# Attention scores in three float32r passes from the second batch on, with scores and exponentials in a tile per head

## The chip, the cores and the metric

The kernel runs on one core of a Trainium2 chip. The metric is the device time of one execution in microseconds (us); lower is better. The core's engines each work through their own queue in order and meet only where one waits for another: TensorE (PE in the rows; PEld is its weight load, which overlaps PE), VectorE (DVE), ScalarE (ACT), GpSimd (POOL), and the queue that issues nearly all DMAs (SP).

## What is computed

Masked attention over 4 batches of 8 heads (576 positions, head size 64), and after it two feed-forward stages over the 2304 tokens, all in float32 with float32 accuracy:

```python
scores = scale * np.matmul(q, k.transpose(0, 1, 3, 2))
thresh = np.max(scores, axis=-1, keepdims=True) - tau
scores = np.where(scores >= thresh, scores, -1e9)
scores = scores - np.max(scores, axis=-1, keepdims=True)
attn = np.exp(scores)
attn = attn / (np.sum(attn, axis=-1, keepdims=True) + 1e-09)
x = np.matmul(attn, v)            # then to (2304, 512)
x = ((x @ w1) * (x @ w2)) @ w3 @ w_out
h = x @ w_in
out = np.maximum(0.01 * h, h) @ w2_out
```

## The kernel before

Two heads are handled together, one in SBUF partitions 0 to 63 and one in 64 to 127. A *unit* is such a pair of heads with about half of its queries: group 0 has 256 queries in 2 steps of 128, group 1 has 320 in 3 steps, of which the first (`c is None`) holds 64 queries of either head in one block through the zero-padded tile `qz`. There are 32 units, 8 to a batch, and 80 steps.

In step `n` the loop at L463 records: `mask(n)` (DVE: keep what lies above the threshold, and sum), `scores(n + 1)` (PE: q times k, two halves of 288 keys for either head, into the PSUM tile `sc`; then, head by head, the negated maximum `nm` and the threshold `th` on DVE and the exponential `e` on ACT), `weighted` for the unit before (PE: `av`), `transposes(n)` (PE: `tp`, `tq` for head 0 and head 1; ACT copies head 0 into `HH`, DVE copies head 1), and `normalise` for the unit before (PE: `bc`; DVE: `xs`; ACT and POOL split `xs` into a float32r pair `x`). Between these stand pieces of a *filler*: `fold_weights` (`ps`, L361) in the first batch, then `gated` (L370) for the group that was finished last, 24 pieces of 12 matmuls: 16 of `psab` (L383), 8 of `psh` (L402). `rate` sets how many pieces a step gets. After the last step come the rest of `gated` and the second feed-forward stage (`up`, `down`).

The feed-forward matmuls take float32 accuracy from three float32r passes over split operands (`PASSES`: high by high, high by low, low by high). The scores, transposes, `av`, `bc` and the folding run in float32; there the compiler makes two instructions of each matmul. A scores matmul uses 64 of the array's 128 rows: head 0 the upper half, head 1 the lower.

What sets the order: PE's is as recorded up to the end of the attention, SP's as recorded up to the middle of batch 1; DVE, ACT, POOL and later SP are ordered by the scheduler. `sc` is a single tile of four PSUM banks for both heads, with one buffer; `e` is one tile for both heads, with two. `scale_unit(u + 1)` runs on DVE in the last step of unit `u`, between `mask(n)` and `scores(n + 1)`. `load_unit(u + 2)` in the first step of unit `u` issues the DMAs of `qk` and `vv`, three buffers each. `ps_w` has two PSUM banks, through which `psab`, `psh`, `av` and `bc` take turns.

Of the kernel before, what the change touches and what calls it, by code (L numbers as in the profile page):

```python
# [33 lines left out]
    (b * 4 + p, g, c) for b in range(B) for g in range(2) for p in range(4) for c in CHUNKS[g])  # L34
NS = len(STEPS)
PASSES = ((0, 0), (0, 1), (1, 0))


@with_exitstack
def attention_gated_ffn(ctx: ExitStack, tc: tile.TileContext, qkv, tau, w3t, wout, w12, w2, out):  # L40
# [32 lines left out]
    nc.vector.memset(sides[D:, D:], 1.0)  # L73
    qz = [cpool.tile([P, P], F32, name=f"qz{i}") for i in range(2)]
    tl = [apool.tile([P, 2, 320], F32, name=f"tl{i}") for i in range(2)]
    for t in (*qz, *tl):
        nc.vector.memset(t, 0.0)
    one = cpool.tile([P, 1], F32, name="one")
    nc.vector.memset(one, 1.0)
# [20 lines left out]
    def stream(jobs, by_dve):  # L100
# [13 lines left out]
        def issue(most=2 * len(jobs)):  # L114

            while len(loaded) < min(most, len(todo)):
                (slot, src, raw), c = todo[len(loaded)]
                if len(loaded) >= state[0] + (7 if raw in ("wB", "wC") else 3):
                    return
                if raw is None:  # L120
                    st = wld.tile([P, 1024], I32, tag="st", name="st", bufs=3)
                    nc.sync.dma_start(out=st, in_=src[:, c * 512:c * 512 + 512].bitcast(I32))
                    loaded.append(st)
                else:
                    if c == 0:
# [37 lines left out]
    def load_unit(u):  # L163

        if u >= len(units):
            return
        pair, g = units[u]
        gq, gw, _ = GROUPS[g]
        b, h = pair // 4, 2 * (pair % 4)
        qk = apool.tile([P, S + 320], F32, tag="qk", name="qk", bufs=3)  # L170
        vv = apool.tile([P, 2, NK, D], F32, tag="vv", name="vv", bufs=3)
        for a in range(2):
            o = a * D
            src = qkv[b, h + a][o:o + D]
            if g == 0:
                nc.sync.dma_start(out=qk[o:o + D, :S + gw], in_=src[:, :S + gw])
            else:
                nc.sync.dma_start(out=qk[o:o + D, :S], in_=src[:, :S])
                nc.sync.dma_start(out=qk[o:o + D, S:], in_=src[:, S + gq:2 * S])
        for a in range(2):  # L180
            nc.sync.dma_start(
                out=vv[:, a], in_=qkv[b, h + a][:, 2 * S:].rearrange("p (c d) -> p c d", c=NK))
        qk_t[u], vv_t[u] = qk, vv

    def scale_unit(u):

        if u >= len(units):
            return
        g = units[u][1]
        qk = qk_t[u]  # L190
        if g:
# [7 lines left out]
            nc.vector.tensor_scalar(out=q, in0=q, scalar1=scl, scalar2=None, op0=ALU.mult))  # L199


    sc_t, e_t, stat = {}, {}, {}

    def scores(n):
# [4 lines left out]
        heads = range(1 if c is None else 2)  # L209
        sc = ps_a.tile([P, 2, 2, 512], F32, tag="sc", name="sc")  # L210
        for half in range(2):
            ks = slice(half * HS, half * HS + HS)
            for a in heads:
                if c is None:
                    nc.tensor.matmul(sc[:, a, half, :HS], qz[u % 2], qk[:, ks], start=True, stop=True)
                else:
                    r = slice(a * D, a * D + D)
                    o = S + Q0[c] - GROUPS[g][0]
                    nc.tensor.matmul(sc[:, a, half, :HS], qk[r, o:o + P], qk[r, ks], start=True, stop=True)  # L219
        e = apool.tile([P, 2, S], F32, tag="e", name="e", bufs=2)  # L220
        ths = []
        for a in heads:
            nm = apool.tile([P, 1], F32, tag="nm", name="nm", bufs=4)
            th = apool.tile([P, 1], F32, tag="th", name="th", bufs=4)
            nc.vector.tensor_reduce(out=nm, in_=sc[:, a, :, :HS], op=ALU.max, axis=AX.XY, negate=True)  # L225
            nc.vector.tensor_scalar(out=th, in0=nm, scalar1=-1.0, scalar2=cb, op0=ALU.mult, op1=ALU.add)
            nc.scalar.activation(  # L227
                e[:, a].rearrange("p (a b) -> p a b", a=2), sc[:, a, :, :HS], AF.Exp, bias=nm)
            ths.append(th)
        sc_t[n], e_t[n] = (sc, ths), e  # L230

    def mask(n):
# [5 lines left out]
        for a, th in enumerate(ths):  # L238
            ev = e_t[n][:, a].rearrange("p (a b) -> p a b", a=2)
            o = 4 if c is None else 2 * (c % 2) + a  # L240
            nc.vector.scalar_tensor_tensor(  # L241
                out=ev, in0=sc[:, a, :, :HS], scalar=th, in1=ev, op0=ALU.is_ge, op1=ALU.mult,
                accum_out=stat[key][:, o:o + 1])
# [3 lines left out]
    def transposes(n):  # L247
# [21 lines left out]
        for a in range(2):  # L269
            tp = ps_a.tile([P, 4, P], F32, tag="tp", name="tp")  # L270
            for kc in range(4):
                nc.tensor.transpose(tp[:, kc], e[:, a, kc * P:kc * P + P], ident)  # L272
# [4 lines left out]
            nc.tensor.transpose(tq[:, a], e[:, a, S - P:], ident)  # L277
            if a:
# [184 lines left out]
    for n in range(NS):  # L463
# [205 lines left out]
```

## Time and profile before

| | |
|---|---|
| median of 3 runs | 1104.95 us (1103.55 to 1105.52) |
| the profiled execution | 1104.54 us, of which the span from first to last instruction is 1102.7 |
| busy share of the span | PE 97%, DVE 46%, ACT 43%, POOL 23% |
| attention | from the start to about 645 us (folding in the first 125 us) |
| end of the gated stage and second feed-forward stage | from there to the end |

A row of a timeline begins with the start in us and the duration in us, then engine, line, operation, output tile, arrow, inputs, shape; in square brackets stands how long the engine had been idle before it and what ended that. Rows that follow one another on one engine are merged, with their count behind an x. A matmul's duration holds its way through the array, so that consecutive ones overlap; what one costs is the distance from start to start.

### The profile page before, as it was taken

To read this page: it belongs to the slowest core of one execution; us is meant where nothing else is said; L and a number is where in the kernel's file an instruction comes from. 1 tells how busy PE (TensorE), PEld (TensorE's weight loads), DVE (VectorE), ACT (ScalarE), POOL (GpSimd) and SP (SyncE) were. 2 spreads that over 40 slices of the span, in tenths; PEclk is the share of its full clock that TensorE was granted. 3 is DMA by queue.
4 is the path that set the end of the run, shared out by engine and by line. 5 is a ranking of instruction groups with operands and counts; after the bars stand their busy time and mean duration, and the time that the engine had idled before them with its cause. 6 is when DMAs were issued, how large, how long until landed. Compare 5 with 4: busy or idle time off the path is not lost.

```text
span 1102.7 us, 16185 instructions
## 1 busy us (share of the span) xinstructions
PE 1065.0 (97%) x6368; PEld 864.2 (78%) x6368; DVE 508.8 (46%) x1087; ACT 474.0 (43%) x891; POOL 256.8 (23%) x256
## 2 busy tenths in 40 slices
PE   7999799999998999999999999999999999999998
PEld 5555487789877888877898789877888888888887
DVE  5767766554666555664556633365311211111111
ACT  4767744343444444443444443477422222222232
POOL 2536712021211120120212146477400100000000
PEclk7999899999999999998999999999999999999999
DMA  9654610312112212111120023356200110010010
GB/s 305 199 198 130 204 54 23 81 35 65 40 40 63 59 30 65 44 54 51 38 62 25 1 79 114 102 191 201 72 13 1 34 34 1 5 44 1 1 39 20
DMA packets 35099, 77.59 MB, mean 70 GB/s; under 512 B 4560, under 2 KB 19408, under 8 KB 32976
## 3 DMA queue, kind: packets, MB, share of 16 engines
q1 hardware_dynamic: 34880, 76.56, 22.0%
q8 instruction: 50, 0.82, 0.3%
q14 instruction: 25, 0.20, 0.1%
q10 hardware_dynamic: 144, 0.00, 0.0%
HBM read 67.11 MB, written 9.44 MB: 69 GB/s over the span
## 4 chain that ended last, share of the span: by engine, by line
PE 81%; DVE 7%; ACT 6%; DMA 2%; issue 2%; POOL 1%; ACTq 0%; SPq 0%; DVEq 0%; POOLq 0%
PE psab L383 16%; PE po L606 16%; PE ps L584 16%; PE psh L402 9%; PE av L294 7%; PE sc L219 7%; PE tp L272 4%; PE ps L361 4%; DVE e L241 2%; ACT e L227 1%; DVE t L145 1%; ACT t L142 1%; PE tq L277 1%; ACT lw L144 1%; ACT HH L276 1%
## 5 line engine op out<-in xcount | busy, mean ns | idle before, releaser
L383 PE MATMUL psab<-x,w 128*128 128x256 f32 (+1 forms) x1536 | 234.5, 303 | 2.9 <-DVE xs L325 2.0
L383 PEld LDWEIGHTS psab<-x,w 128*128 128x128 f32 x1536 | 208.9, 189 | 24.9 <-issue 15.9
L584 PE MATMUL ps<-h,w 128*128 128x512 f32 (+1 forms) x960 | 215.7, 370 | 0.4 <-POOL w L153 0.3
L606 PE MATMUL po<-w,gg 128*128 128x512 f32 x864 | 213.8, 392 | 1.8 <-ACT gg L591 1.8
L584 PEld LDWEIGHTS ps<-h,w 128*128 128x128 f32 x960 | 169.0, 188 | 36.3 <-POOL w L153 1.3
L606 PEld LDWEIGHTS po<-w,gg 128*128 128x128 f32 x864 | 159.2, 188 | 38.1 <-ACT gg L591 3.3
L592 DVE TENSOR_TENSOR gg<-gf,gg 128x512 fp32r<-128x512 f32 (+1 forms) x80 | 61.2, 765 | 270.0 <-ACT gg L591 268.4
L225 DVE TENSOR_REDUCE nm<-sc 128x1 f32<-128x576 f32 x144 | 108.8, 756 | 108.3 <-PE sc L219 66.7
L227 ACT ACTIVATE e<-sc,nm 128x576 f32<-128x576 f32 x144 | 107.0, 743 | 117.3 <-DVE nm L225 117.0
L589 ACT ACTIVATE gf<-ps 128x512 f32<-128x512 f32 (+1 forms) x80 | 44.2, 554 | 227.0 <-PE ps L584 227.0
L241 DVE SCALAR_TENSOR_TENSOR e<-sc,th,e 128x576 f32<-128x576 f32 x144 | 112.7, 815 | 46.5 <-ACT e L227 46.5
L402 PE MATMUL psh<-gt,w 128*128 128x256 f32 (+1 forms) x768 | 115.1, 301 | 0.6 <-ACT ht L409 0.5
L394 POOL TENSOR_TENSOR gt<-at,gt 128x256 fp32r<-128x256 f32 (+1 forms) x64 | 52.7, 824 | 264.3 <-ACT gt L393 264.3
L402 PEld LDWEIGHTS psh<-gt,w 128*128 128x128 f32 x768 | 104.1, 189 | 7.7 <-issue 5.4
L219 PE MATMUL sc<-qk 64*128 64x288 f32 x512 | 81.7, 438 | 15.1 <-DVE e L241 11.2
L272 PE MATMUL tp<-ident,e 128*128 128x128 f32 x512 | 79.1, 278 | 6.0 <-ACT HH L276 6.0
L272 PEld LDWEIGHTS tp<-ident,e 128*128 128x128 f32 x512 | 61.9, 143 | 16.2 <-ACT HH L276 8.5
L151 POOL TENSOR_TENSOR lw<-t,lw 128x512 int32<-128x512 int32 x48 | 66.0, 1380 | 25.6 <-ACT lw L144 15.2
L219 PEld LDWEIGHTS sc<-qk 64*128 64x128 f32 x512 | 44.9, 188 | 33.9 <-issue 9.5
L294 PE MATMUL av<-HH,vv 128*64 128x256 f32 (+1 forms) x512 | 69.8, 416 | 0.0
L561 POOL TENSOR_TENSOR h<-hr,h 128x1024 fp32r<-128x1024 f32 (+1 forms) x10 | 23.8, 2380 | 188.2 <-DVE h L560 188.2
L361 PE MATMUL ps<-wo,w 128*128 128x512 f32 x128 | 60.0, 614 | 5.3 <-DVE xs L325 4.7
(72 smaller groups left out, 989.0 us busy)
## 6 DMA issues: line engine op xcount, KB each, us to landing
st<-in_w SPq DMA_DIRECT2D x40, 512.0 KB, 4.6
vv<-in_qkv SPq DMA_DIRECT2D x64, 160.0 KB, 2.4
raw<-in_w3t SPq DMA_DIRECT2D x8, 1024.0 KB, 5.8
qk<-in_qkv SPq DMA_DIRECT2D x32, 208.0 KB, 3.5
qk<-in_qkv SPq DMA_DIRECT2D x32, 144.0 KB, 3.0
out<-os SPq DMA_DIRECT2D x18, 256.0 KB, 2.1
raw<-in_wout SPq DMA_DIRECT2D x4, 1024.0 KB, 11.3
raw<-in_w SPq DMA_DIRECT2D x4, 1024.0 KB, 6.2
```

What stands on the lines that cost most here:

```text
L151: nc.gpsimd.tensor_tensor(out=lw, in0=t, in1=lw, op=ALU.add)
L219: nc.tensor.matmul(sc[:, a, half, :HS], qk[r, o:o + P], qk[r, ks], start=True, stop=True)
L225: nc.vector.tensor_reduce(out=nm, in_=sc[:, a, :, :HS], op=ALU.max, axis=AX.XY, negate=True)
L227: nc.scalar.activation(e[:, a].rearrange("p (a b) -> p a b", a=2), sc[:, a, :, :HS], AF.Exp, bias=nm)
L241: nc.vector.scalar_tensor_tensor(out=ev, in0=sc[:, a, :, :HS], scalar=th, in1=ev, op0=ALU.is_ge, op1=ALU.mult, accum_out=stat[key][:, o:o ...
L272: nc.tensor.transpose(tp[:, kc], e[:, a, kc * P:kc * P + P], ident)
L294: nc.tensor.matmul(av[a * D:a * D + D, :gw], vv[:, a, kc], rhs, start=(i == 0), stop=(i == NK - 1))
L361: nc.tensor.matmul(ps, w3_t[i][:, j * P:j * P + P], wo_t[j // 2][:, (j % 2) * 512:(j % 2) * 512 + 512], start=(j == 0), stop=(j == KF - 1))
L383: nc.tensor.matmul(ps[:, :gw], w12_t[i][:, a, mat * 512 + kk * P:mat * 512 + kk * P + P], xt[kk][:, c, :gw], start=(m == 0), stop=(m == 11))
L402: nc.tensor.matmul(ps[:, :gw], w34_t[i // 2][:, a, i % 2, o * P:o * P + P], gt[i][:, c, :gw], start=(m == 0), stop=(m == 23))
L584: nc.tensor.matmul(ps[:, :tw], w2_t[j][:, a, kk * P:kk * P + P], h3_t[ci][:, c, kk, :tw], start=(m == 0), stop=(m == 11))
L606: nc.tensor.matmul(po_t[t], gg[:, c, t * P:t * P + P], w2_t[j][:, a, 512:], start=(j == 0 and (a, c) == PASSES[0]), stop=(j == KF2 - 1 and ...
```

## The change

- `sc` and `e` become one tile per head (`sc0`, `sc1` with two banks each; `e0`, `e1`).
- Units 0 to 7 (batch 0) compute scores as before. From unit 8 on, the scores are three float32r passes: `split_unit(u + 1)`, recorded in the first step of unit `u` behind `scores(n + 1)`, scales q on DVE, copies k and q to the float32r tile `qkh` on ScalarE, subtracts to `qkl` on VectorE, and for group 1 makes four 64x64 copies into `qzs`. `scale_unit` does nothing for these units.
- `qkh` and `qkl` share the ring `st` of the weight stage, which goes from 3 buffers to 4. `xpool` goes from 8 to 6, `vv` from 3 to 2 (loaded by `load_v`, one unit later than before), and `hr` is loaded in four pieces of 512 columns a chunk instead of two of 1024. `qz` moves to another pool.

The diff without the unchanged surroundings and the purely mechanical renames:

```diff
+PER = 8
-    xpool = ...tc.tile_pool(name="xpool", bufs=8, reuse_waits="tile"))
+    xpool = ...tc.tile_pool(name="xpool", bufs=6, reuse_waits="tile"))
-    qz = [cpool.tile([P, P], F32, name=f"qz{i}") for i in range(2)]
+    qz = [apool.tile([P, P], F32, name=f"qz{i}") for i in range(2)]
+    qzs = [apool.tile([P, 2, P], F32R, name=f"qzs{i}") for i in range(2)]
+    for t in qzs:
+        nc.vector.tensor_copy(t, tl[0][:, :, :P])
-                    st = wld.tile([P, 1024], I32, tag="st", name="st", bufs=3)
+                    st = wld.tile([P, 1024], I32, tag="st", name="st", bufs=4)
...
+    def load_v(u):
...
+        vv = vv_t[u] = apool.tile([P, 2, NK, D], F32, tag="vv", name="vv", bufs=2)
...
     def scale_unit(u):
-        if u >= len(units):
+        if u >= PER:
             return
...
+    def split_unit(u):
+        if not PER <= u < len(units):
+            return
+        g = units[u][1]
+        n = S + GROUPS[g][1]
+        qk = qk_t[u]
+        q = qk[:, S:n]
+        tc.keep_in_program_order(
+            nc.vector.tensor_scalar(out=q, in0=q, scalar1=scl, scalar2=None, op0=ALU.mult))
+        hi = wld.tile([P, 1024], F32R, tag="st", name="qkh", bufs=4)
+        lo = wld.tile([P, 1024], F32R, tag="st", name="qkl", bufs=4)
+        nc.scalar.copy(hi[:, :n], qk[:, :n])
+        nc.vector.tensor_tensor(out=lo[:, :n], in0=qk[:, :n], in1=f(hi[:, :n]), op=ALU.subtract)
+        qks_t[u] = (hi, lo)
+        if g:
+            for i, part in enumerate((hi, lo)):
+                for a in range(2):
+                    r = slice(a * D, a * D + D)
+                    nc.vector.tensor_copy(qzs[u % 2][r, i, r], part[r, S:S + D])
...
-        sc = ps_a.tile([P, 2, 2, 512], F32, tag="sc", name="sc")
+        sc = [ps_a.tile([P, 2, 512], F32, tag=f"sc{a}", name="sc") for a in heads]
+        if u < PER:
+            parts, qzu = (qk,), qz[u % 2].unsqueeze(1)
+        else:
+            parts, qzu = qks_t[u], qzs[u % 2]
+        passes = PASSES[:1] if u < PER else PASSES
         for half in range(2):
             ks = slice(half * HS, half * HS + HS)
-            for a in heads:
...
+            for i, (x, y) in enumerate(passes):
+                for a in heads:
+                    if c is None:
+                        lhs, rhs = qzu[:, x], parts[y][:, ks]
+                    else:
+                        r = slice(a * D, a * D + D)
+                        o = S + Q0[c] - GROUPS[g][0]
+                        lhs, rhs = parts[x][r, o:o + P], parts[y][r, ks]
+                    nc.tensor.matmul(
+                        sc[a][:, half, :HS], lhs, rhs, start=(i == 0), stop=(i == len(passes) - 1))
-        e = apool.tile([P, 2, S], F32, tag="e", name="e", bufs=2)
+        e = [apool.tile([P, S], F32, tag=f"e{a}", name="e", bufs=2) for a in heads]
...
             scores(n + 1)
+        if n and STEPS[n - 1][:2] != (pair, g):
+            split_unit(u + 1)
...
         if n == 0 or STEPS[n - 1][:2] != (pair, g):
+            load_v(u + 1)
             load_unit(u + 2)
...
-        for o in range(0, KD, 2):
-            hr = p2.tile([P, 2, 512], F32, tag="hr", name="hr")
+        for o in range(KD):
+            hr = p2.tile([P, 512], F32, tag="hr", name="hr")
```

PE, at the turn from batch 2 to batch 3, in the one step of a batch for which the filler has run out (`tp`, `tq`: transposes; `bc`: normalise; `sc`: scores of the next step; `av`: weighted). Before:

```order
L402 MATMUL psh<-gt,w_813 128x256 x6
L402 MATMUL psh<-gt,w_1013 128x256 x6
L272 MATMUL tp<-ident,e 128x128 x4
L277 MATMUL tq<-ident,e 128x128
L272 MATMUL tp<-ident,e 128x128 x4
L277 MATMUL tq<-ident,e 128x128
L322 MATMUL bc<-pairs,rb 128x64
L324 MATMUL bc<-ident,rb 128x128 x2
L219 MATMUL sc<-qk 128x288 x4
L294 MATMUL av<-tl_95,vv 64x256 x2
```

The same place after the change:

```order
L313 MATMUL tp<-ident,e 128x128 x4
L318 MATMUL tq<-ident,e 128x128
L363 MATMUL bc<-pairs,rb 128x64
L365 MATMUL bc<-ident,rb 128x128 x2
L259 MATMUL sc<-qkh 128x288 x2
L259 MATMUL sc<-qkl,qkh 128x288 x2
L259 MATMUL sc<-qkh,qkl 128x288 x2
L259 MATMUL sc<-qkh 128x288 x2
L259 MATMUL sc<-qkl,qkh 128x288 x2
L259 MATMUL sc<-qkh,qkl 128x288 x2
L335 MATMUL av<-tl_95,vv 64x256 x2
```

Nothing has moved around the scores; their four matmuls (eight instructions) have become twelve single ones, and the two of each row are head 0 and head 1.

DVE at the turn from batch 1 to batch 2, the step without filler and the one ahead of it (`nm`, `th`, `e,stat`: maximum, threshold and mask of a head; `rr`: reciprocals; `HH`: the copy of head 1's transposes). Before:

```order
L241 SCALAR_TENSOR_TENSOR e,stat<-sc,th,e 128x576 x2
L199 TENSOR_SCALAR qk<-qk,scl 128x256
L305 TENSOR_SCALAR rr<-stat 128x4
L306 RECIPROCAL rr<-rr 128x4
L274 COPY HH<-tp 128x4x128
L225 TENSOR_REDUCE nm<-sc 128x1
L226 TENSOR_SCALAR th<-nm,cb 128x1
L225 TENSOR_REDUCE nm<-sc 128x1
L226 TENSOR_SCALAR th<-nm,cb 128x1
L274 COPY HH<-tp 128x4x128
L241 SCALAR_TENSOR_TENSOR e,stat<-sc,th,e 128x576 x2
L325 TENSOR_TENSOR xs<-xs,bc 128x320
```

After, the same two steps:

```order
L267 TENSOR_SCALAR th<-nm,cb 128x1 x2
L222 TENSOR_SCALAR qk<-qk,scl 128x256
L282 SCALAR_TENSOR_TENSOR e,stat<-sc,th,e 128x576 x2
L226 TENSOR_TENSOR qkl<-qk,qkh 128x832
L346 TENSOR_SCALAR rr<-stat 128x4
L347 RECIPROCAL rr<-rr 128x4
L315 COPY HH<-tp 128x4x128
L266 TENSOR_REDUCE nm<-sc 128x1 x2
L267 TENSOR_SCALAR th<-nm,cb 128x1 x2
L282 SCALAR_TENSOR_TENSOR e,stat<-sc,th,e 128x576 x2
L315 COPY HH<-tp 128x4x128
L366 TENSOR_TENSOR xs<-xs,bc 128x320
```

The two maxima now stand side by side, the masks stand ahead of the copy of head 1, and the subtraction `qkl` stands behind the masks of the step before.

SP at the end of the attention (`st`: weights of the second stage; `hr`: the first chunk of its input). Before:

```order
L410 DMA h3d<-ht 128x256 x3
L559 DMA hr<-h3d 128x2x512
L122 DMA st<-in_w 128x1024 x2
L410 DMA h3d<-ht 128x256
L559 DMA hr<-h3d 128x2x512
```

After:

```order
L126 DMA st<-in_w 128x1024 x4
L451 DMA h3d<-ht 128x256 x3
L604 DMA hr<-h3d 128x512
L126 DMA st<-in_w 128x1024 x2
L451 DMA h3d<-ht 128x256
L604 DMA hr<-h3d 128x512
L126 DMA st<-in_w 128x1024 x2
L604 DMA hr<-h3d 128x512
```

The first loads of `st`, which before were issued early in the attention, now stand at its end, and the input comes in smaller pieces.

## Rows read from the trace of the kernel before

**Rows 1.** First part of the page: busy time, share of the span, instructions.
```profile
PE 1065.0 (97%) x6368; PEld 864.2 (78%) x6368; DVE 508.8 (46%) x1087; ACT 474.0 (43%) x891; POOL 256.8 (23%) x256
```

**Rows 2.** Busy time by stretch; then granted clock, DMA share, GB/s.
```profile
core 0: us, PE busy (x) PEld busy (x) DVE busy (x) ACT busy (x) POOL busy (x), PEclk, DMA share, GB/s
...
200.00:250.00 50.00, 47.68 (x336) 39.42 (x335) 27.74 (x65) 21.00 (x41) 9.39 (x12) 0.97 0.25 68
...
500.00:550.00 50.00, 47.68 (x327) 39.27 (x328) 26.88 (x63) 19.95 (x40) 9.39 (x12) 0.93 0.13 37
```

**Rows 3.** Waits of PE: for whom, us in total, times, longest.
```profile
PE sc L219 <- DVE e L241: 11.2, 8, 2.5
PE tp L272 <- ACT HH L276: 6.0, 7, 2.2
...
PE psab L383 <- DVE xs L325: 2.0, 8, 0.3
```

**Rows 4.** Timeline of PE at the turn from batch 2 to batch 3.
```profile
501.46 1.24 PE L219 MATMUL sc<-qk 64*128 64x288 f32 x8
502.63 1.70 PE L402 MATMUL psh<-gt,w 128*128 128x256 f32 x12
...
505.45 0.66 PE L272 MATMUL tp<-ident,e 128*128 128x128 f32 x4 [0.57 <-ACT HH L276]
...
506.22 0.39 PE L324 MATMUL bc<-ident,rb 128*128 128x128 f32 x2
508.36 2.29 PE L219 MATMUL sc<-qk 64*128 64x288 f32 x8 [1.75 <-DVE e L241]
```

**Rows 5.** Timelines of DVE and of ACT in the same step.
```profile
502.75 0.76 DVE L225 TENSOR_REDUCE nm<-sc 128x1 f32<-128x576 f32 x1 [2.02 <-PE sc L219]
...
504.32 0.76 DVE L225 TENSOR_REDUCE nm<-sc 128x1 f32<-128x576 f32 x1 [0.56 <-ACT e L227]
...
506.14 0.69 DVE L274 COPY HH<-tp 128x512 f32<-128x512 f32 x1 [0.82 <-PE tp L272]
506.75 0.81 DVE L241 SCALAR_TENSOR_TENSOR e<-sc,th,e 128x576 f32<-128x576 f32 x1
...
507.48 0.81 DVE L241 SCALAR_TENSOR_TENSOR e<-sc,th,e 128x576 f32<-128x576 f32 x1
...
505.29 0.75 ACT L227 ACTIVATE e<-sc,nm 128x576 f32<-128x576 f32 x1
```

**Rows 6.** Timeline in batch 1, a step ahead of a 64-query step.
```profile
298.03 1.22 PE L215 MATMUL sc<-qk,qz 128*128 128x288 f32 x4
...
298.96 0.48 DVE L325 TENSOR_TENSOR xs<-xs,bc 128x320 f32<-128x320 f32 x1
...
299.50 1.70 PE L383 MATMUL psab<-x,w 128*128 128x256 f32 x12 [0.25 <-DVE xs L325]
```

**Rows 7.** Full-height matmuls: float32 (timeline), float32r (chain that ended last).
```profile
98.17 3.60 PE L361 MATMUL ps<-wo,w 128*128 128x512 f32 x8
...
671.75 14.35 PE psab L383 x96
```

**Rows 8.** DVE and ACT operations nearest to the added ones (timeline; groups).
```profile
657.27 0.68 DVE L153 TENSOR_TENSOR w<-lw,w 128x512 fp32r<-128x512 f32 x1
...
L327 ACT CAST x<-xs 128x320 fp32r<-128x320 f32 x14 | 6.4, 460 | 25.4 <-DVE xs L325 25.1
L327 ACT CAST x<-xs 128x256 fp32r<-128x256 f32 x12 | 4.9, 407 | 13.3 <-DVE xs L325 13.3
...
L194 DVE TENSOR_SCALAR qz<-qk,scl 64x64 f32<-64x64 f32 x26 | 6.4, 248 | 0.4
```

**Rows 9.** Timelines of DVE and POOL behind the attention: the input's first chunk.
```profile
656.66 0.69 DVE L560 CAST h<-hr 128x1024 fp32r<-128x1024 f32 x1 [2.39 <-DMA hr<-h3d]
...
664.35 1.42 DVE L560 CAST h<-hr 128x1024 fp32r<-128x1024 f32 x1 [1.54 <-DMA hr<-h3d]
...
657.49 2.75 POOL L561 TENSOR_TENSOR h<-hr,h 128x1024 fp32r<-128x1024 f32 x1 [0.79 <-DVE h L560]
```

More of the change, by code (lines that the diff above doesn't have):

```diff
@@ L59, in attention_gated_ffn @@
     s_att = ExitStack()
-    xpool = s_ffn.enter_context(tc.tile_pool(name="xpool", bufs=8, reuse_waits="tile"))
+    xpool = s_ffn.enter_context(tc.tile_pool(name="xpool", bufs=6, reuse_waits="tile"))
     s_ld = ExitStack()
@@ L170, in load_unit @@
         qk = apool.tile([P, S + 320], F32, tag="qk", name="qk", bufs=3)
-        vv = apool.tile([P, 2, NK, D], F32, tag="vv", name="vv", bufs=3)
         for a in range(2):
@@ L179, in load_unit @@
                 nc.sync.dma_start(out=qk[o:o + D, S:], in_=src[:, S + gq:2 * S])
+        qk_t[u] = qk
+    def load_v(u):
+        if u >= len(units):
+            return
+        pair = units[u][0]
+        b, h = pair // 4, 2 * (pair % 4)
+        vv = vv_t[u] = apool.tile([P, 2, NK, D], F32, tag="vv", name="vv", bufs=2)
         for a in range(2):
@@ L182, in load_unit @@
                 out=vv[:, a], in_=qkv[b, h + a][:, 2 * S:].rearrange("p (c d) -> p c d", c=NK))
-        qk_t[u], vv_t[u] = qk, vv
     def scale_unit(u):
-        if u >= len(units):
+        if u >= PER:
             return
@@ L199, in scale_unit @@
             nc.vector.tensor_scalar(out=q, in0=q, scalar1=scl, scalar2=None, op0=ALU.mult))
+    qks_t = {}
+    def split_unit(u):
+        if not PER <= u < len(units):
+            return
+        g = units[u][1]
[14 more added lines that the diff above has]
+                    nc.vector.tensor_copy(qzs[u % 2][r, i, r], part[r, S:S + D])
     sc_t, e_t, stat = {}, {}, {}
@@ L209, in scores @@
         heads = range(1 if c is None else 2)
-        sc = ps_a.tile([P, 2, 2, 512], F32, tag="sc", name="sc")
+        sc = [ps_a.tile([P, 2, 512], F32, tag=f"sc{a}", name="sc") for a in heads]
[4 more added lines that the diff above has]
+        passes = PASSES[:1] if u < PER else PASSES
         for half in range(2):
             ks = slice(half * HS, half * HS + HS)
-            for a in heads:
[L214 to L219, printed above, removed]
-        e = apool.tile([P, 2, S], F32, tag="e", name="e", bufs=2)
+            for i, (x, y) in enumerate(passes):
[9 more added lines that the diff above has]
+        e = [apool.tile([P, S], F32, tag=f"e{a}", name="e", bufs=2) for a in heads]
         ths = []
@@ L224, in scores @@
             th = apool.tile([P, 1], F32, tag="th", name="th", bufs=4)
-            nc.vector.tensor_reduce(out=nm, in_=sc[:, a, :, :HS], op=ALU.max, axis=AX.XY, negate=True)
+            nc.vector.tensor_reduce(out=nm, in_=sc[a][:, :, :HS], op=ALU.max, axis=AX.XY, negate=True)
             nc.vector.tensor_scalar(out=th, in0=nm, scalar1=-1.0, scalar2=cb, op0=ALU.mult, op1=ALU.add)
             nc.scalar.activation(
-                e[:, a].rearrange("p (a b) -> p a b", a=2), sc[:, a, :, :HS], AF.Exp, bias=nm)
+                e[a].rearrange("p (a b) -> p a b", a=2), sc[a][:, :, :HS], AF.Exp, bias=nm)
             ths.append(th)
@@ L238, in mask @@
         for a, th in enumerate(ths):
-            ev = e_t[n][:, a].rearrange("p (a b) -> p a b", a=2)
+            ev = e_t[n][a].rearrange("p (a b) -> p a b", a=2)
             o = 4 if c is None else 2 * (c % 2) + a
             nc.vector.scalar_tensor_tensor(
-                out=ev, in0=sc[:, a, :, :HS], scalar=th, in1=ev, op0=ALU.is_ge, op1=ALU.mult,
+                out=ev, in0=sc[a][:, :, :HS], scalar=th, in1=ev, op0=ALU.is_ge, op1=ALU.mult,
                 accum_out=stat[key][:, o:o + 1])
@@ L260, in transposes @@
             for kc in range(4):
-                nc.tensor.transpose(tp[:, kc], e[:, 0, kc * P:kc * P + P], ident)
-            nc.tensor.transpose(tq[:, 0], e[:, 0, S - P:], ident)
+                nc.tensor.transpose(tp[:, kc], e[0][:, kc * P:kc * P + P], ident)
+            nc.tensor.transpose(tq[:, 0], e[0][:, S - P:], ident)
             nc.scalar.copy(HH[:, :, :, :D], tp.rearrange("p k (a w) -> p k a w", a=2))
@@ L271, in transposes @@
             for kc in range(4):
-                nc.tensor.transpose(tp[:, kc], e[:, a, kc * P:kc * P + P], ident)
+                nc.tensor.transpose(tp[:, kc], e[a][:, kc * P:kc * P + P], ident)
             if a:
@@ L276, in transposes @@
                 nc.scalar.copy(HH[:, :, a, o:o + P], tp)
-            nc.tensor.transpose(tq[:, a], e[:, a, S - P:], ident)
+            nc.tensor.transpose(tq[:, a], e[a][:, S - P:], ident)
             if a:
@@ L425, in attention_gated_ffn @@
     issue(2)
+    load_v(0)
     load_unit(1)
@@ L555, in load_h3 @@
         hh = pool.tile([P, 2, KD, 512], F32R, tag=f"h3{ci % 2}", name="h3", bufs=1)
-        for o in range(0, KD, 2):
-            hr = p2.tile([P, 2, 512], F32, tag="hr", name="hr")
-            hv = hr[:, :, :tw]
-            nc.sync.dma_start(out=hv, in_=h3d[o:o + 2, :, t0:t0 + tw].rearrange("o p t -> p o t"))
-            nc.vector.tensor_copy(hh[:, 0, o:o + 2, :tw], hv)
+        for o in range(KD):
+            hr = p2.tile([P, 512], F32, tag="hr", name="hr")
+            hv = hr[:, :tw]
+            nc.sync.dma_start(out=hv, in_=h3d[o, :, t0:t0 + tw])
+            nc.vector.tensor_copy(hh[:, 0, o, :tw], hv)
             nc.gpsimd.tensor_tensor(
-                out=hh[:, 1, o:o + 2, :tw], in0=hv, in1=f(hh[:, 0, o:o + 2, :tw]), op=ALU.subtract)
+                out=hh[:, 1, o, :tw], in0=hv, in1=f(hh[:, 0, o, :tw]), op=ALU.subtract)
         h3_t[ci] = hh
```

## The prediction, made before the changed kernel ran

> **What bounds the kernel now.** I read the page's busy times first, then the stretches, then PE's waits, and last the timelines around the longest of them. The page says that PE is busy for 97% of the span, and no other engine for half of it [rows 1]: time is saved where PE's instructions get shorter, or where PE stands idle or slow. In the attention's later batches DVE is busy 27.7 us of 50, ACT 21.0 [rows 2], so work added there can hide unless PE waits for just that instruction. PE's own waits are short but sit at fixed places [rows 3]: 11.2 us in 8 waits of the scores for a mask, 6.0 us of the transposes for a copy, 2.0 us in 8 of `psab` for `xs`. The timelines show why. At the turn of a batch the filler is used up; PE then has only transposes and `bc`, which are done at 506.6, and stands until 508.36, because the next scores overwrite `sc`, which the masks still read [rows 4]. The masks are that late because the two heads go one after the other: the second maximum waits for the exponential of the first (504.32, idle 0.56 behind ACT), the second exponential runs from 505.29 to 506.04, a copy stands ahead of the masks at 506.14, and the second mask ends at 508.3 [rows 5]. Both stretches with PE at 47.7 of 50 us hold such a turn, and in both the granted clock is below one, 0.97 and 0.93 [rows 2].
>
> **The change part by part.** All sums go against the profiled execution's 1104.54 us.
>
> *Scores of two heads, 48 steps.* A step's eight instructions take 1.17 us from start to start of the next (501.46 to 502.63) [rows 4]. Full-height float32 needs 3.60 us for eight instructions over 512 columns [rows 7], 0.45 each; that is two clocks a column at 2.4 GHz (0.427) and a tail, so 0.24 for 288 columns. Eight one after the other would be 1.92; 1.17 is four times 0.24 and 0.21. So the two heads, on either half of the array, run side by side, and I read the 0.21 as the change from full to half height and back. After the change there are six such pairs. Full-height float32r takes 14.35 us for 96 instructions over 320 columns [rows 7], 0.149 each including the tail, where one clock a column is 0.133; that gives 0.12 for 288 columns with nothing on top and 0.136 with it. I take 0.135, as the nearest row is a real stream: 6 x 0.135 + 0.21 = 1.02, 0.15 less than 1.17, **-7.2 us** in 48 steps. With 0.12 it is -11.5; the other end is the third rival.
>
> The Trainium skill ("FP8 and Floating Point Precision", TensorE Precision Notes) counts four passes for true float32, against the three passes here. By that ratio the 0.96 becomes 0.72, which is -11.5 us and a total of 1083; the float32r row with its 0.015 on top is why I stay above it.
>
> *Scores of 64 queries, 12 steps.* Four full-height float32 instructions of 0.24 become six of 0.135: -0.15 each, **-1.8 us**. Behind them `psab` waits for `xs`, 0.25 us each time [rows 6]; the eight waits make 2.0 us [rows 3]. DVE loses the two `qz` scalings of 0.248 us [rows 8] and a `scale` ahead of `xs` there, and its masks come earlier, so I take the six of batches 1 to 3 as gone: **-1.5 us** (0 if DVE fills the room otherwise).
>
> *One tile per head.* The maximum of head 1 needs no exponential any more, and the order shows both maxima, both thresholds, both masks and only then the copy. In the step of [rows 5]: first maximum at 502.6 (the scores are 0.15 shorter), second to 504.2, its exponential to 504.95, masks to 506.1. ACT copies head 0's transposes only behind both exponentials, so the second group of transposes starts at 505.6 and not 505.45, and `bc` ends at 506.75. The scores start there in place of 508.36: 1.6 us, of which 0.15 is counted above. What is late next is that copy on ACT, not DVE. Three turns: **-4.4 us**. Of the 11.2 us the turns are 3 x 1.75, and the longest single wait is 2.5, in the first steps, where I count nothing. The other four hold 3.5 us and are each shorter than what the masks gain (about 1.5): **-3.0 us**.
>
> *Clock.* 0.97 and 0.93 of 50 us are 1.5 and 3.5 us of lost array time [rows 2], behind the turns' idle stretches; the level there is 1.2 GHz. With idle times of about 0.9 us in place of 0.57 + 1.75 [rows 4] I expect most of it back: **-3.0 us** (0 to -5.0).
>
> *Splitting k and q, 24 units.* The nearest DVE subtraction takes 0.68 us for 512 columns [rows 8], so at most 1.1 and 1.2 us for 832 and 896. Four 64x64 copies cost up to 4 x 0.248, the two scalings they replace are saved. That is +1.1 us (group 0) and +1.7 us (group 1) a unit. ACT's cast grows by 53 ns in 64 columns, 407 to 460 [rows 8], hence 0.9 us. In all 34 us on DVE and 22 us on ACT, an eighth more for DVE in the attention. They stand behind masks and exponentials that PE needs, and ahead of `rr`, the product of `psab` and the copy of head 1. PE has `av` and a filler piece there, and DVE was idle 2.02 us before the next maximum [rows 5]. With all of it hidden the cost is 0, with all exposed 34; I take 0.1 a unit, **+2.4 us**. The scaling itself leaves the path between the last mask of a unit and the next unit's scores.
>
> *Smaller rings.* `vv` waits for the same `weighted` as before, now ahead of `qk` on SP; `qk` is wanted a unit later, so nothing waits. `xpool` with 6 holds a group of four and two of the next; the third is written when two thirds of `gated`, hence all of `psab`, are through. `st` is now held by `qkh` and `qkl`, so the first loads for the second stage move from early on to the end of the attention; SP's pieces of the input stand behind them. That input took 7.7 us from cast to cast for 1024 columns [rows 9]: about 4 of DMA, 0.7 of cast, 2.75 of POOL. Four half pieces repeat the DMA, up to 8 us more until the last, while PE has `psab` between: **+1.0 us** (0 to 8). The first batch keeps its instructions; 0 there, give or take 3.
>
> *Sum:* -7.2 -1.8 -1.5 -4.4 -3.0 -3.0 +2.4 +1.0 = -17.5, so 1087.0 for the profiled execution; the median of the runs lies 0.4 above that, **1087.4 us**.
>
> **The rivals.** *The waits stay* (the scheduler's order or ACT's copy holds PE all the same, so the tile per head doesn't do what it says): -7.2 -1.8 +3.4 gives 1098.9, with the median's 0.4 **1099**. Against it: the order has the masks ahead of the copy. *DVE becomes what PE waits for* in the split's steps: half of 1.4 us exposed in 24 units is 16.8 in place of 2.4, **1102**. For it speaks the unbroken block of two maxima, scaling, two masks, subtraction; against it the idle time of DVE. *Half-height float32r doesn't run side by side*: no row shows two such instructions at one clock a column. Twelve at 0.135 and 0.21 are 1.83 a step, +31.7 us in place of -7.2, so **1126**, slower. It decides from a pair of 0.196 us on, where 48 x (6 x 0.196 + 0.21 - 1.17) uses up the other gains of 10.3. Against it: float32 pairs do run side by side. *A pair's weights load only when the pair before is through.* An unhidden load is bounded by half of the 0.21, 0.105; pairs of 0.24 make 1.65 a step, +23, **1118**, slower. Against it: four pairs with four such loads would take 1.38 us already now, not 1.17. The Trainium skill states this rule ("TensorE: Matmul & The Clock Gate", Part 3): a weight load overlaps running matmuls only of another row group. By that rule 1118 would come out; the trace of before disagrees for float32, and only float32r's shorter pair could bring it back.
>
> **How the numbers follow.** Forecast 0.66 (1079 to 1095 by itself), waits stay 0.10, DVE 0.12, no overlap 0.08, weight loads 0.04. The low end is every gain at its full size (-11.5 -2 -2 -5 -3.5 -5, no cost: 1076), trimmed by a microsecond; the high end takes in the waits that stay and about half of the DVE case: 1077 to 1101. What can be told from no change is 0.2%, 2.2 us. Faster: the forecast, the staying waits and most of the DVE case, 0.85; same: 0.04; slower: 0.11.
>
> **What would show it.** Scores of a step at about 1.02 us from start to start: right; 1.65 or 1.83: the rivals. The second maximum without a wait for ACT; the wait of the scores for masks down from 11.2 to about 3 us; a granted clock near one at the turns. New waits of `psab` or transposes for DVE's line 226 or of scores for a `qkl`: the DVE rival. The forecast is wrong above all if the pairs are longer than 0.16 us, or if PE meets DVE in each unit.

## The result and the profile after

The changed kernel takes 1069.82 us (median of 4 runs, 1069.58 to 1070.22), the kernel before 1104.25 us on the same chip: a ratio of 0.969, interval 0.967 to 0.971. It is faster by 34.4 us; 17.5 had been forecast, and the time lies below the range of 1077 to 1101. The profiled execution's span is 1068.4 us, 34.3 less than before.

The first part of the page after, busy time by engine (against [rows 1]):

```profile
PE 1042.7 (98%) x6584; PEld 866.4 (81%) x6584; DVE 520.7 (49%) x1147; ACT 490.5 (46%) x915; POOL 259.4 (24%) x266
```

Stretches after, columns as in [rows 2]. The turn from batch 2 to batch 3 now lies in the one from 450 on, and the first turn ends ahead of 200, so that the other two hold none:

```profile
200.00:250.00 50.00, 50.00 (x388) 46.29 (x387) 28.89 (x72) 23.62 (x47) 11.02 (x14) 1.00 0.17 49
450.00:500.00 50.00, 48.92 (x409) 42.36 (x405) 33.46 (x82) 24.94 (x48) 7.61 (x11) 1.00 0.20 59
500.00:550.00 50.00, 50.00 (x391) 45.37 (x391) 31.07 (x79) 23.63 (x45) 9.26 (x14) 1.00 0.16 49
```

PE is busy all through two of them, and for 48.92 us of the one with a turn (47.68 before); the granted clock is 1.00 in each, where 0.97 and 0.93 stood. PE's waits after (against [rows 3]):

```profile
PE tp L313 <- ACT HH L317: 12.0, 8, 2.4
...
PE psab L424 <- DVE at L432: 0.8, 2, 0.4
...
PE sc L259 <- DVE e L282: 0.3, 1, 0.3
```

The scores' wait for a mask is gone, 11.2 us to 0.3, and so is that of `psab` for `xs`. The transposes wait longer for ACT's copy than before, 12.0 us in place of 6.0: it is what comes late next. The timeline of PE at the turn from batch 2 to batch 3 shows both (against [rows 4]):

```profile
476.82 0.40 PE L259 MATMUL sc<-qkh 64*128 64x288 f32 x2
477.06 0.30 PE L259 MATMUL sc<-qkl,qkh 64*128 64x288 f32 x2
477.20 0.29 PE L259 MATMUL sc<-qkh,qkl 64*128 64x288 f32 x2
...
477.60 0.29 PE L259 MATMUL sc<-qkh,qkl 64*128 64x288 f32 x2
477.82 1.70 PE L443 MATMUL psh<-gt,w 128*128 128x256 f32 x12
...
481.14 0.66 PE L313 MATMUL tp<-ident,e 128*128 128x128 f32 x4 [1.08 <-ACT HH L317]
...
482.24 0.40 PE L259 MATMUL sc<-qkh 64*128 64x288 f32 x2
```

From scores to scores this step takes 5.42 us (476.82 to 482.24) where [rows 4] have 6.90. The scores start straight behind `bc`; the idle time left, 1.08 us, stands ahead of head 1's transposes. DVE and ACT in the same step (against [rows 5]):

```profile
477.92 1.42 DVE L266 TENSOR_REDUCE nm<-sc 128x1 f32<-128x576 f32 x2 [1.83 <-PE sc L259]
...
479.57 0.82 DVE L282 SCALAR_TENSOR_TENSOR e<-sc,th,e 128x576 f32<-128x576 f32 x1
...
480.65 0.82 DVE L282 SCALAR_TENSOR_TENSOR e<-sc,th,e 128x576 f32<-128x576 f32 x1 [0.25 <-ACT e L268]
...
481.84 0.69 DVE L315 COPY HH<-tp 128x512 f32<-128x512 f32 x1 [0.36 <-PE tp L313]
...
478.72 0.74 ACT L268 ACTIVATE e<-sc,nm 128x576 f32<-128x576 f32 x1 [2.84 <-DVE nm L266]
...
479.87 0.75 ACT L268 ACTIVATE e<-sc,nm 128x576 f32<-128x576 f32 x1
480.50 0.59 ACT L317 COPY HH<-tp 128x512 f32<-128x512 f32 x1
```

The two maxima stand side by side, the second without the 0.56 us behind ACT that it had in [rows 5], and the masks end at 481.5, three quarters of a microsecond ahead of the scores that need their room. ACT copies head 0's transposes only behind both exponentials, at 480.50.

**Where the 34 us are.** The start of a step's scores, step by step, in the two traces (read from the first `sc` matmul of each step):

| stretch | before, us | after, us | difference | forecast |
|---|---|---|---|---|
| start to step 20 (batch 0) | 184.27 | 176.56 | -7.7 | 0 |
| steps 20 to 40 (batch 1) | 151.50 | 142.87 | -8.6 | |
| steps 40 to 60 (batch 2) | 149.87 | 142.87 | -7.0 | |
| steps 60 to 79 (batch 3) | 145.82 | 135.93 | -9.9 | |
| batches 1 to 3 together | 447.2 | 421.7 | -25.5 | -18.5 |
| step 79 to the end | 471.3 | 470.2 | -1.1 | +1.0 |

Batch 2 can be split without a remainder: each of its 20 steps is shorter by 0.16 to 0.20 us, 0.18 in the mean (-3.6), and four by more on top of that: the first one by 0.91, the turn by 1.31, the two 64-query steps whose `psab` waited by 0.61 and 0.57. Batches 1 and 3 have the same and one step more, the one behind the turn, which is shorter by a further 1.63 and 3.07 us: that is the clock. Stretches of the kernel before behind its three turns, columns as in [rows 2]:

```profile
206.00:219.00 13.00, 12.01 (x76) 9.31 (x78) 6.45 (x18) 4.38 (x9) 1.74 (x2) 0.87 0.22 62
358.00:368.50 10.50, 10.02 (x74) 8.41 (x74) 5.94 (x16) 4.05 (x8) 1.56 (x2) 1.00 0.26 75
508.00:522.00 14.00, 13.64 (x78) 10.22 (x80) 5.82 (x16) 4.58 (x9) 1.74 (x2) 0.76 0.21 57
```

0.13 of 13 us are 1.7, 0.24 of 14 are 3.4, and behind the turn of batch 2 nothing was lost; after the change nothing is in any of the three.

The first steps show where batch 0 gains. DVE and PE in step 0 and at the scores of step 1, before:

```profile
8.92 0.76 DVE L225 TENSOR_REDUCE nm<-sc 128x1 f32<-128x576 f32 x1 [0.56 <-ACT e L227]
...
10.49 0.82 DVE L241 SCALAR_TENSOR_TENSOR e<-sc,th,e 128x576 f32<-128x576 f32 x1 [0.56 <-ACT e L227]
...
12.20 1.59 PE L219 MATMUL sc<-qk 64*128 64x288 f32 x8 [2.46 <-DVE e L241]
```

and after:

```profile
8.24 0.75 DVE L266 TENSOR_REDUCE nm<-sc 128x1 f32<-128x576 f32 x1
8.90 0.81 DVE L282 SCALAR_TENSOR_TENSOR e<-sc,th,e 128x576 f32<-128x576 f32 x1
...
9.86 0.72 PE L259 MATMUL sc<-qk 64*128 64x288 f32 x2 [0.15 <-DVE th L267]
```

The first mask ends 1.6 us earlier, and head 0's scores, which need only their own tile, start 2.3 us earlier. Step 2 starts at 16.14 in place of 22.31, step 5 at 42.35 in place of 48.58. There is no filler yet that could stand in such a gap. A second wait goes with it, which [rows 3] leave out: that of the scores for the next unit's scaled q, which DVE scales behind both masks. Before and after:

```profile
PE sc L219 <- DVE qk L199: 3.9, 3, 2.5
```

```profile
PE sc L259 <- DVE qk L209: 0.5, 1, 0.5
```

Of the 7.7 us of batch 0, 6.2 stand in steps 0 to 4, 0.4 around the end of the folding, and 1.1 in two 64-query steps, where `psab` waited for `xs` as it did in the later batches.

### The profile page after: what moved, and what is told of

Read it like the earlier page. It is cut to its first block, busy times and chain, and to the rows that moved or that the text cites. A ratio compares the mean times of both kernels' runs of the same rounds, so it can differ in the third digit from the quotient of the medians.

```text
span 1068.4 us, 16904 instructions
## 1 busy us (share of the span) xinstructions
PE 1042.7 (98%) x6584; PEld 866.4 (81%) x6584; DVE 520.7 (49%) x1147; ACT 490.5 (46%) x915; POOL 259.4 (24%) x266
## 4 chain that ended last, share of the span: by engine, by line
PE 88%; ACT 4%; DVE 3%; issue 2%; POOL 1%; DMA 1%; ACTq 0%; SPq 0%; POOLq 0%; DVEq 0%
PE psab L424 18%; PE po L651 17%; PE ps L629 17%; PE psh L443 10%; PE av L335 7%; PE sc L259 7%; PE tp L313 5%; PE ps L402 3%; DVE t L149 1%; PE tq L318 1%; ACT t L146 1%; ACT lw L148 1%; DMA hr<-h3d 1%; ACT e L268 1%; POOL lw L155 1%
## 5 line engine op out<-in xcount | busy, mean ns | idle before, releaser
L629 PEld LDWEIGHTS ps<-h,w 128*128 128x128 f32 x960 | 169.2, 188 | 36.6 <-ACT w L154 2.2
L637 DVE TENSOR_TENSOR gg<-gf,gg 128x512 fp32r<-128x512 f32 (+1 forms) x80 | 58.6, 733 | 256.1 <-ACT gg L636 254.5
L268 ACT ACTIVATE e<-sc,nm 128x576 f32<-128x576 f32 x144 | 102.5, 742 | 87.9 <-DVE nm L266 87.7
L266 DVE TENSOR_REDUCE nm<-sc 128x1 f32<-128x576 f32 x144 | 103.2, 753 | 76.7 <-PE sc L259 76.7
L313 PEld LDWEIGHTS tp<-ident,e 128*128 128x128 f32 x512 | 60.6, 140 | 21.7 <-ACT HH L317 14.5
L155 POOL TENSOR_TENSOR lw<-t,lw 128x512 int32<-128x512 int32 x48 | 66.8, 1395 | 27.2 <-DVE t L149 16.8
L606 POOL TENSOR_TENSOR h<-hr,h 128x512 fp32r<-128x512 f32 (+1 forms) x20 | 26.0, 1298 | 191.6 <-DVE h L605 191.6
L315 DVE COPY HH<-tp 128x512 f32<-128x512 f32 x64 | 44.1, 688 | 48.2 <-PE tp L313 47.4
L335 PE MATMUL av<-HH,vv 128*64 128x256 f32 (+1 forms) x512 | 67.5, 406 | 0.0
L149 DVE TENSOR_SCALAR t<-t 128x512 int32<-128x512 int32 x72 | 52.4, 728 | 20.4 <-ACT t L146 20.1
```

The source lines that it names most:

```text
L155: nc.gpsimd.tensor_tensor(out=lw, in0=t, in1=lw, op=ALU.add)
L266: nc.vector.tensor_reduce(out=nm, in_=sc[a][:, :, :HS], op=ALU.max, axis=AX.XY, negate=True)
L268: nc.scalar.activation(e[a].rearrange("p (a b) -> p a b", a=2), sc[a][:, :, :HS], AF.Exp, bias=nm)
L313: nc.tensor.transpose(tp[:, kc], e[a][:, kc * P:kc * P + P], ident)
L335: nc.tensor.matmul(av[a * D:a * D + D, :gw], vv[:, a, kc], rhs, start=(i == 0), stop=(i == NK - 1))
L629: nc.tensor.matmul(ps[:, :tw], w2_t[j][:, a, kk * P:kk * P + P], h3_t[ci][:, c, kk, :tw], start=(m == 0), stop=(m == 11))
```

## The experiments

Theory: two causes that add up. The shared tile made the heads go one after the other, and PE waited for that wherever no filler covers it, in the first batch too; and the passes are cheap because half-height pairs run side by side. Rivals: the start's gain is the clock's, or the loads' (rings); the split is not hidden; the pairs owe nothing to running side by side.

**One tile per head alone.** The kernel before with

```diff
-        sc = ps_a.tile([P, 2, 2, 512], F32, tag="sc", name="sc")
+        sc = [ps_a.tile([P, 2, 512], F32, tag=f"sc{a}", name="sc") for a in heads]
-        e = apool.tile([P, 2, S], F32, tag="e", name="e", bufs=2)
+        e = [apool.tile([P, S], F32, tag=f"e{a}", name="e", bufs=2) for a in heads]
```

> The kernel before with scores and exponentials in a tile per head, nothing else changed (float32 scores, old rings, old loads). Theory T (the gain that I did not forecast comes from the shorter chain of a step, at the start of the kernel above all): batch 0 begins its successor (step 20) at about 177 us in place of 184.3, and the turns' and 64-query waits go too: about 20 us faster than before, 1084. Rival R (batch 0 gains from the loads' new order and the smaller rings): batch 0 keeps its 184.3, only about 13 us come from turns, waits and clock, 1091.

1081.58 us, ratio 0.980 [0.978, 0.981]. Step 20 starts at 176.60, as with the whole change (176.56): the gain of batch 0 comes with the tiles alone. A two-head step's scores still take 1.171 us. Its waits of PE:

```profile
PE tp L272 <- ACT HH L276: 11.3, 8, 2.4
```

The wait of the scores for masks is down to 0.3 us in this run as well. Steps 40, 54, 57 and the turn are shorter by 0.91, 0.61, 0.57 and 1.54 us, and the step behind the third turn by 3.07: the clock comes back with the tiles, too.

**The passes alone**, the whole change with `sc` and `e` as in the kernel before:

> The changed kernel with one tile for both heads again, for the scores and for the exponentials; the three passes, the split and the rings stay. Theory T: only the scores' shorter stream is left, 48 x 0.18 + 12 x 0.18 = 10.8 us, perhaps 2 us more from the scaling that left the path: 1091 to 1094, and step 20 starts near 184 as before. Rival R: step 20 starts near 177, 1085.

1089.53 us, 0.988 [0.986, 0.990], 1.5 below the range expected. Step 20 starts at 184.47, as before the change, and the masks' wait is back:

```profile
PE sc L259 <- DVE e L282: 11.8, 9, 2.5
```

Its steps 54 and 57 are shorter by 0.75 and 0.67, of which 0.18 are the scores: either half of the change takes most of `psab`'s wait away by itself, 3.5 us in six steps with the tiles and 3.1 with the passes, where the expectation had perhaps 2 for the scaling. What it did not have is the clock: in this trace it fell behind the second and the third turn and cost 1.5 us each, in place of 1.63 and 3.07 behind the first and the third. The parts make 22.3 + 13.5 + 0.8 = 36.6 us by their ratios (with the next run) and the whole 34.4: what both halves take counts twice, though the intervals hardly tell 2.2 us from nothing.

**The rings alone**, the kernel before with the changed pools and loads (`xpool` 6, `vv` 2, `st` 4, `load_v`, `hr` in pieces of 512):

> The kernel before with the new rings and loads alone (xpool 6, vv 2 and loaded a unit later, st 4, the second stage's input in four pieces, qz in the other pool); float32 scores, one tile for both heads. Theory T: within 2 us of before, 1103 to 1105. Rival R: 6 to 8 us faster, with step 20 near 177 us.

1102.71 us, 0.9993 [0.998, 1.001]: nothing that can be told from no change. Step 20 starts at 182.88, 1.4 us earlier than before; all of that is in step 1, where the clock stayed full (the last run comes back to this).

**The passes head by head**, the whole change with

```diff
-        for half in range(2):
-            ks = slice(half * HS, half * HS + HS)
-            for i, (x, y) in enumerate(passes):
-                for a in heads:
+        for a in heads:
+            for half in range(2):
+                ks = slice(half * HS, half * HS + HS)
+                for i, (x, y) in enumerate(passes):
```

> The changed kernel with the scores' matmuls written head by head (all of head 0, then all of head 1), so that neighbours use the same half of the array. If two heads run side by side and this is what makes 0.99 us a step, twelve instructions now come one after the other at 0.12 to 0.135 each: 1.65 to 1.85 us a step, +31 to +41 us in 48 steps of batches 1 to 3, and in the 16 float32 steps of batch 0 up to +0.96 each, partly hidden there; head 0's maximum starts earlier, which takes little back: 1100 to 1120. If the hardware overlaps neighbours of one half as well, it stays at 1070.

1089.56 us, 0.988 [0.986, 0.989], 19.7 us more than the whole change: in sign as expected, in size too little. A step's scores take 1.367 us, not 1.65 or more. The timeline of PE shows why:

```profile
483.17 0.39 PE L259 MATMUL sc<-qkh 64*128 64x288 f32 x1
483.41 0.29 PE L259 MATMUL sc<-qkl,qkh 64*128 64x288 f32 x1
483.53 0.29 PE L259 MATMUL sc<-qkh,qkl 64*128 64x288 f32 x1
483.54 0.41 PE L259 MATMUL sc<-qkh 64*128 64x288 f32 x2
483.78 0.31 PE L259 MATMUL sc<-qkl,qkh 64*128 64x288 f32 x2
483.91 0.31 PE L259 MATMUL sc<-qkh,qkl 64*128 64x288 f32 x2
484.05 0.29 PE L259 MATMUL sc<-qkh 64*128 64x288 f32 x1
```

Head 0 has six instructions to run, and head 1's first starts right behind head 0's third (483.54 behind 483.53; the x2 there is this one and head 0's fourth). From there three slots hold two, and head 1 ends alone. Nine slots of 0.13 us are taken in place of twelve or six. That the two halves work at the same time is thereby shown, and that the order in which they are written costs 0.37 us a step, 17.7 in 48. The turn alone is 0.14 us shorter, because its wait for ACT's copy is 0.57 us in place of 1.08. Step 20 starts 4.5 us later than with the whole change: step 1 is 3.6 longer, since head 1's scores wait 1.10 us for a mask there and the clock is at 0.66 from 10 to 20 us (1.00 with the whole change); the rest comes about the end of the folding, where a wait for `xs` takes 5.2 us in place of 3.3.

**Which of the two tiles?** The kernel before with only `sc` in a tile per head, and with only `e`:

> The kernel before with the scores' PSUM tile per head, the exponentials still in one tile. If the second head's maximum waited because both heads' scores share a tile (it and the first exponential only read it), nearly all of the 21.9 us of the tile per head comes back: 1081 to 1085. If the shared exponential tile is what ties the heads together, nothing does: 1102 to 1105.

> The kernel before with the exponentials in a tile per head, the scores still in one PSUM tile. The mirror of the run with the scores' tile alone: 1102 to 1105 if the shared scores tie the heads, 1081 to 1085 if the shared exponentials do.

`sc` alone: 1080.93 us, 0.978 [0.976, 0.981], step 20 at 176.11; all of the gain, to within the intervals. `e` alone: 1103.60 us, 0.9996 [0.998, 1.001]; PE waits as in the kernel before:

```profile
PE sc L219 <- DVE e L241: 10.5, 8, 1.8
```

So it is the PSUM tile. Head 1's maximum on DVE and head 0's exponential on ACT both only read it, in different banks, and still the one ran behind the other as long as they named one tile. The profile shows the wait; what in the making of the program put it there, no run shows.

**The subtraction twice**, the whole change with

```diff
         nc.vector.tensor_tensor(out=lo[:, :n], in0=qk[:, :n], in1=f(hi[:, :n]), op=ALU.subtract)
+        nc.vector.tensor_tensor(out=lo[:, :n], in0=qk[:, :n], in1=f(hi[:, :n]), op=ALU.subtract)
```

> The changed kernel with the subtraction of every split done twice (24 more VectorE instructions of 832 or 896 columns, about 1 us each by their row). My forecast put 0.1 us a unit on the path for the whole split. If the split lies beside PE's work as the trace of after suggests, 24 us more on VectorE cost 0 to 3 us: 1070 to 1073. If VectorE is at its limit, up to 24: 1080 to 1094.

1070.15 us, 0.969 [0.967, 0.971], against 1069.82: another 25 us on DVE cost 0.3 or nothing. DVE's part of the split is hidden with room to spare. ACT's part, 21.7 us of copies, was not doubled; that nothing of it is exposed either is seen in batch 2 of the whole change, where every step is shorter by about the same 0.18 us, those with a split too. The split's rows on DVE in the whole change, groups by line and shape:

```profile
L226 DVE TENSOR_TENSOR qkl<-qk,qkh 128x896 fp32r<-128x896 f32 x12 | 13.1, 1088 | 0.0
L226 DVE TENSOR_TENSOR qkl<-qk,qkh 128x832 fp32r<-128x832 f32 x12 | 12.3, 1022 | 0.0
...
L232 DVE CAST qzs<-qkl 64x64 fp32r<-64x64 f32 x24 | 4.5, 189 | 0.3
L232 DVE CAST qzs<-qkh 64x64 fp32r<-64x64 f32 x24 | 4.5, 186 | 0.2
```

**Filler left for the turn**, the whole change with

```diff
-            rate, due = (1.22, 1.55)[gg], 0.0
+            rate, due = (1.15, 1.55)[gg], 0.0
```

> The changed kernel with the filler's rate for group 0 at 1.15 in place of 1.22, so that pieces are left for the turn's step. There PE now waits 1.08 us for ScalarE's copy at each of the three turns. If those waits come from the filler having run out, 3 us go: about 1067. If the copy is late in any case, or the pieces left over only move, 1069 to 1071.

1067.44 us, 0.966 [0.965, 0.968], 2.4 less than the whole change, and the fastest version here. Its waits of PE for ACT's copy:

```profile
PE tp L313 <- ACT HH L317: 8.3, 5, 2.4
```

The three waits of 1.08 us at the turns are gone; the five left lie in the first batch. The profiled spans differ by 3.2 us. Batches 1 to 3 give 1.3 us each, 3.9 in all, with as many matmuls as before in each. The first batch is 1.4 shorter (step 20 at 175.17) and the part behind step 79 2.1 longer, because one piece of 12 matmuls has moved from the one to the other: `gated` starts at 119.8 us, inside the first batch, and behind step 79 there are 216 matmuls of `psab` in place of 204. So the turns give more than the 3 us expected, and the piece that was moved costs 0.7 at the end.

**The clock at the start.** In the kernel before the granted clock fell at the start; with 24 small matmuls in place of 7 behind each of the first three steps it does not:

```diff
-            keep_busy(7)
+            keep_busy(24)
```

> The kernel before with 24 in place of 7 of the small matmuls that keep TensorE busy in each of the first three steps; nothing else changes. What is asked is which part of the 7 us that the start gave back with a tile per head belongs to the clock, which fell to half for two stretches of 6.8 us within the first 30 us of the kernel before and for one of 3.4 us in the kernel after. If the chain of a step sets the start (the second head's scores wait for e of the first), the extra matmuls fill idle time only: the scores of step 5 begin at 47 to 49 us (48.6 in the kernel before) and the time is 1103 to 1105. If the half clock sets it, the scores of step 5 begin at 42 to 45.5 and the time is 1098 to 1101.

1105.52 us, 1.002 [1.001, 1.004]. Stretches of the kernel before (first two lines) and of this one; the clock is the third number from the end:

```profile
10.00:20.00 10.00, 7.17 (x32) 5.72 (x32) 5.76 (x12) 6.00 (x11) 2.54 (x2) 0.66 1.04 370
20.00:30.00 10.00, 6.85 (x32) 5.64 (x32) 7.37 (x20) 6.19 (x11) 3.43 (x4) 0.66 0.81 274
```

```profile
10.00:20.00 10.00, 7.25 (x61) 6.62 (x62) 6.72 (x15) 7.36 (x13) 3.58 (x3) 1.00 1.04 372
20.00:30.00 10.00, 9.29 (x78) 8.21 (x78) 7.52 (x19) 7.00 (x13) 4.80 (x6) 1.00 0.98 327
```

The clock stays full, and step 1 starts at 12.18 all the same (12.20 before). From step 2 on this run tells little: the small matmuls now fill the room ahead of the scores of steps 2, 3 and 4 up to their start, 5.4 to 5.7 us each time, and so set that start themselves.

```profile
15.29 5.52 PE L453 MATMUL scratch<-ident 128*128 128x128 f32 x48
20.95 1.24 PE L219 MATMUL sc<-qk 64*128 64x288 f32 x8
```

Step 2 starts at 20.95 (22.31 before), step 3 at 29.51 (30.11), and step 5 at 50.25, later than either theory had it. The run with the rings alone settles what this one leaves open. It has one tile for both heads and no more small matmuls than before, and its clock stayed full through step 1:

```profile
10.00:20.00 10.00, 4.26 (x32) 3.44 (x32) 6.80 (x15) 7.24 (x13) 3.59 (x3) 1.00 1.02 378
```

```profile
20.89 1.38 PE L225 MATMUL sc<-qk 64*128 64x288 f32 x8 [3.89 <-DVE qk L205]
```

There PE stands idle for 3.89 us ahead of step 2, and from step 1 to step 2 it takes 8.72 us, as in the run with `e` alone; it was 10.11 in the kernel before and is 6.28 after the change. Of the 6.2 us that the first two steps gained, 1.4 are thereby the clock's and 4.8 those of the chain of a step.

## Why the prediction was right in sign and half in size

**The step that failed** is the last of its sum: "The first batch keeps its instructions; 0 there, give or take 3." It keeps its instructions, but not their order: the tile per head holds in batch 0 as well. The rows for it were there. The prediction names the longest wait of the scores for a mask, 2.5 us, "in the first steps, where I count nothing", and it is the very wait that it removed at the turns. It does not name the wait for the scaled q, 3.9 us, which shrank to 0.5, nor the two `psab` waits in the first batch. The runs put -7.7 us there, nearly half of the 16.8 by which the sum fell short, and all of it comes with the PSUM tile (`sc` alone: step 20 at 176.11 in place of 184.27).

**The other terms**, from the steps' lengths:

| term | forecast | measured | how |
|---|---|---|---|
| scores of two heads | -7.2 | -8.6 | 48 x 0.18 |
| 64-query scores | -1.8 | -2.2 | 12 x 0.18 |
| `psab` for `xs` | -1.5 | -3.5 | 6 x 0.59 |
| turns | -4.4 | -3.9 | 3 x 1.31 |
| other score waits | -3.0 | -2.7 | 3 x 0.91 |
| clock | -3.0 | -4.7 | 1.63 + 3.07 |
| split of k and q | +2.4 | 0 | subtraction twice costs 0.3 at most |
| rings, tail | +1.0 | -0.9 | behind step 79, less its own scores; the rings alone and the tiles alone each have -0.9 there too |
| first batch | 0 | -7.7 | |

The measured ones make -34.2, the difference of the spans but for rounding. The mechanism was right for each of the first six, and right in detail at the turn: "What is late next is that copy on ACT, not DVE", with 1.08 us of idle time where about 0.9 was expected. The size of the clock term is in part luck: the kernel before lost 1.63 and 3.07 us behind the first and the third turn in this trace, the run of the passes alone 1.5 behind the second and the third.

*The pairs.* They follow one another at 0.133 us (0.13 or 0.14 in the rows, 477.06 to 477.60 for four), where 0.135 was taken, and the change to half height and back costs 0.19 (0.99 from start to start less 6 x 0.133), where 0.21 was taken. Both small errors went the same way. By the Trainium skill's count of four passes for true float32 ("FP8 and Floating Point Precision", TensorE Precision Notes) the 0.96 would have become 0.72, an estimate; the trace has 6 x 0.133 = 0.80, nearer to the row of [rows 7] than to that ratio.

*`psab` for `xs`.* The prediction priced this wait at the 0.25 us in the bracket of [rows 6]. The bracket counts from the end of the last matmul's way through the array; what is lost counts from start to start. Before, `psab` starts 1.47 us after the first of four score matmuls (298.03 to 299.50), which need 0.96. After:

```profile
283.96 0.30 PE L259 MATMUL sc<-qkh,qzs 128*128 128x288 f32 x1
...
284.62 0.30 PE L259 MATMUL sc<-qkh,qzs 128*128 128x288 f32 x1
284.75 1.58 PE L424 MATMUL psab<-x,w 128*128 128x256 f32 x12
```

0.79 us, six times 0.13. The gap was 0.5 us, twice what the bracket said, and 0.57 to 0.61 with the rest of the step.

*The split.* Its size was somewhat smaller than worked out: it adds 34.4 us on DVE (13.1 + 12.3 + 4.5 + 4.5), and the `qz` scalings fell from 10.0 to 3.4, so 28 net, where 34 were taken with that saving counted. Its price was not right: by the doubled subtraction nothing of it is exposed, and DVE is idle for about 20 us in 50 even now. The 0.1 us a unit rested on no row.

*The range.* Its low end took every gain at full size and each cost at zero, but no gain in the first batch, although "give or take 3" was written there. With the 7.7 the sum of its low end would have been 1068.

**The rivals.** *The waits stay:* no; 11.2 us became 0.3. *DVE becomes what PE waits for:* no, by the doubled subtraction. *No side by side:* no, by the pairs of x2, and by the run head by head. *A pair's weights load only when the pair before is through:* no; 288 columns at one clock each and 2.4 GHz are 0.120 us, and the pairs lie 0.133 apart, which leaves 0.013 for a load that is not hidden. The loads for the pair at 477.20 start with the pair at 477.06:

```profile
477.06 0.19 PEld L259 LDWEIGHTS sc<-qkh,qkl 64*128 64x128 f32 x2
```

The Trainium skill's rule for weight loads ("TensorE: Matmul & The Clock Gate", Part 3) would have given pairs of about 0.24, by the prediction's estimate; this trace does not bear it out for half-height float32r.

## What to carry to other kernels

In this kernel two readers of one PSUM tile ran one behind the other, although they read different banks of it: where two engines work on two halves of such a tile, try a tile for each half before shortening anything else (here 22 of the 34 us, with no instruction fewer; the same for the SBUF tile of the exponentials gave nothing). Look for a removed wait everywhere the code runs, above all where no filler stands, and price it by the distance from start to start, not by the idle time in the bracket. Write half-height matmuls in alternation, and leave some filler for the one step that has none.

## What the runs showed of the hardware beside that

Written head by head, head 1's first instruction started right behind head 0's third (483.54 us), although three more of head 0 stand ahead of it in the order of the kernel, so that a step took 1.367 us, between the 0.99 of alternation and the twelve single slots of 0.133 with the change of height on top (1.79). In float32 no such difference showed: head by head, a step of the first batch took 1.178 us where 1.171 stood. And a clock kept full with small matmuls bought nothing at the start: TensorE ran at 1.00 in place of 0.66 between 10 and 30 us, step 3 began 0.6 us earlier and step 5 1.7 later.
